# A planner's durations replaced from one point on, and the last attention of a fused fp32 kernel built like its first

## The chip, the cores and the metric

The kernel runs on one core of one Trainium2 chip. The core has a matmul engine (TensorE, PE in the profile, with its weight loads shown apart as PEld), a vector engine (VectorE, DVE), a scalar engine (ScalarE, ACT), GpSimd (POOL) and SyncE (SP), which here issues transfers. Each engine works through its own instructions strictly in order and waits on semaphores for the others. The metric is the device time of one execution in microseconds (us); a lower one is better.

## The reference, cut to what matters

Three layers in fp32, for 2 batches of 448 positions and a model width of 768. The first is causal attention with 12 heads of width 64; the second an MLP with spatial gating; the third, called the last attention here, has 4 experts, each a causal attention head of width 64 of its own, of which each position takes the best two, weighted by a gate.

```python
# first attention, per batch and head
a = exp(scores - max); a = a / (sum(a) + 1e-9); x = a @ v
# gated MLP
h = gelu(x @ w_in); u, v = halves of h;  v_n = layernorm(v) * g_ln
v_s = einsum('ts,bsd->btd', w_sg, v_n) + b_sg
x = x + (u * v_s) @ w_out
# last attention
logits = x @ w_gate;  w = softmax over the 2 largest logits
for e in range(4):
    q, k, v = x @ wq[e], x @ wk[e], x @ wv[e]
    a = causal softmax of q @ k.T / 8
    ye = a @ v @ wo[e]
    out += (w of e, 0 where e isn't among the two) * ye
```

## The kernel before, in words

**Precision.** Big products are made of three: an fp32 number is split into a high half, which the fast fp32r path of the matmul engine takes exactly (xh, gh, wqh), and a low half, the rest (xl, gl, wql); hi x hi + hi x lo + lo x hi are added up in PSUM (`mm3`, L820). `halves` (L613) makes the pair: a copy into hi (L371 on ACT, L373 on DVE or L375 on POOL) and a subtraction into lo (L378, on DVE or POOL). Scores and the first attention's products are plain fp32 matmuls.

**Stages.** The first attention fills the first part of the span. Then come the v chains (x @ w_in for the half that is normalised) and u chains (L859), the spatial product (`spatial`, L1042: 8 tiles of four matmuls at L1053, then on each tile a DVE step with gain and bias at L1056, a multiplication by u at L1059, which DVE or POOL may do, and the halves gh, gl), the product with w_out (`wout_chain`, L1065: 12 tiles of 12 matmuls, then on each a sum with the residual's high half at L1074 on DVE, with its low half at L1077 on DVE or POOL, and the halves of the new x, again xh, xl), and the last attention: `proj_v` (values and gate logits together, 260 columns), `proj_qk`, `scores3` (L1302; two heads side by side, two banks each), the softmax of a bank, the product with v, and `wo_chain` (L1341) with the output transfers.

**The two attentions differ.** `bank_chain` (L417) serves both. Of a bank of scores it takes masked negated scores and their row minimum on DVE (L427), then exp on ACT (L437). In the first attention (`split` false) exp also sums each row; POOL adds 1e-9 (L443), DVE takes the reciprocal (L445), DVE or POOL scales P (L449, L451), the matmul engine transposes the four 128 x 128 blocks (L455), a copy brings them to SBUF (L458), and `pair_chain` (L481) multiplies with v as weight (L497), which gives y already transposed, for two heads in one PSUM tile. In the last attention (`split` true) P is cut into two fp16 halves, `pn` (POOL L471, DVE L473), a DMA transposes both (`dma_start_transpose`, L476) into `pt`, and `out_chain` (L509) multiplies with P as weight and v in fp16 halves with a column of ones for the row sums (L516, L518, L520: 30 matmuls a head). It is normalised and gated in PSUM (L531 to L547), and `y_split` (L551) transposes y back on the matmul engine (L557) and makes its halves. v for it is scaled by its largest element (`v_scales`, L567, with a matmul by a matrix of ones at L576) and split (`v_split`, L593).

**What sets the order.** A planner in Python (`class Order`) builds the instruction streams. A piece of work is a chain of `Step`s; each step has a cost for every engine that may do it (from functions such as `vec(n)`, `pool2(n)` at L61 to L82), marks that it needs and buffers that it takes from rings. `begin` picks for each step the engine on which it would end first by these costs, plus a bias per engine (`BIAS`, and `LATE` after the planned time `TURN`, L221); `run` emits the step that can start first, with the ranks in `R` (L276) deciding between steps within a slack of 60 ns. So costs, biases and ranks decide both which engine does a step and where it stands in that engine's queue.

Of the kernel before, what the change touches and what calls it, by code (L numbers as in the profile page):

```python
# [12 lines left out]
F16 = mybir.dt.float16  # L13
# [5 lines left out]
P = 128  # L19
B, H, S, D = 2, 12, 448, 64  # L20
DM = 768
# [6 lines left out]
PSC = 2.0 ** 14  # L28
MASK = -8.0e9
VW = 132  # L30

SLOTS = ((0, 3, 1, 2), (3, 0, 2, 1))
FLIPS = ((1, 0, 3, 1, 1), (2, 4, 2, 2, 2), (3, 3, 1, 1, 3), (0, 5, 1, 1, 1), (4, 5, 1, 1, 2), (4, 7, 1, 1, 3), (0, 7, 0, 1, 0))
# [4 lines left out]

# [9 lines left out]
TERMS = [  # L50
    (1, 0, 0, 1), (1, 0, 1, 0), (2, 0, 1, 4), (2, 0, 2, 1), (2, 0, 3, 2),
    (0, 1, 0, 0), (3, 1, 0, 4), (3, 1, 1, 1), (3, 1, 2, 2), (3, 1, 3, 3),
]
# [6 lines left out]

def act(n, sb=True, ap=False):  # L61
    return (94 if sb else 51) + 93 * ap + n / 1.2


def mm(n):
    return 2 + n / 2.4


def vec(n):
    return 69 + n / 0.96  # L70


def vec2(n):
    return 69 + n / 1.92


def pool1(n):
    return 56 + n / 0.96


def pool2(n):
    return 150 + 2.1 * n  # L82
# [20 lines left out]
def dma_t(ns, take=(), need=()):  # L103
    return Step({"S": 1244}, take, need, ns, 625)


# [4 lines left out]
class Order:  # L111
# [13 lines left out]
    LATE = dict(T=0, A=300, V=700, G=-300, S=0, Z=0)  # L125
    TURN = 190000
# [68 lines left out]
    def begin(self, ch):  # L195
# [13 lines left out]
        for e, c in st.cost.items():  # L209
# [11 lines left out]
            bias = self.LATE[e] if t > self.TURN else self.BIAS[e] * min(1.0, t / 20000)  # L221
# [55 lines left out]
    PV=(564, 568), PV0=569.5, vp=(569.5, 557.4), gt=(557.3, 543.0), QK=(555.5, 558.9, 570, 579.5),  # L277
    S=(552.4, 561, 560.3, 566.6), WO=(665.7, 669.3), WO0=669, v=(511, 517), v0=509, sp=(526, 538.7),
# [14 lines left out]
def attention_moe_kernel(  # L293
# [21 lines left out]

    uid = [0]
# [19 lines left out]
    ones128 = ct([P, P], F32, "ones128")  # L336
    V.memset(ones128, 1.0)
# [51 lines left out]
    def subs(n):  # L389
        return dict(V=vec(n), G=pool2(n))  # L390


    class Core:


        def __init__(self, stack, side, n, np32, npn, npt):
# [8 lines left out]
            self.split = npn > 0  # L405
            if npn:
                ring("pn" + n, [ct([P, 1024], F16, f"pn{n}{i}", pool) for i in range(npn)])
                ring("pt" + n, [ct([P, 8, P], F16, f"pt{n}{i}", pool) for i in range(npt)])
            else:
                ring("pt" + n, [ct([P, 8, P], F32, f"pt{n}{i}", pool) for i in range(npt)])  # L410
                ring("sm" + n, [ct([P, 4], F32, f"sm{n}{i}", pool) for i in range(4)])
                for _, _, t in o.rings["sm" + n]:
                    G.memset(t, 1.0)
            ring("bias" + n, [ct([P, 4], F32, f"bias{n}{i}", pool) for i in range(6)])
            ring("r" + n, [ct([P, 4, 1], F32, f"r{n}{i}", pool) for i in range(4)])

    def bank_chain(c, key, bank, s, pts, pt_of=None):  # L417
# [7 lines left out]
        _, tm, bias = yield op(V=690, take=("tm" + c.n, "bias" + c.n))  # L425
# [6 lines left out]
        if not c.split:  # L432
            _, p32, sm = yield op(A=1000, take=("p32" + c.n, "sm" + c.n))
        else:
            _, p32 = yield op(A=800, take=("p32" + c.n,))
        for n, (i, rs, cs) in enumerate(parts):
            A.activation(p32[rs, cs], tm[rs, cs], AF.Exp, bias=bias[rs, i : i + 1], scale=-1.0,  # L437
                         **({} if c.split else dict(accum_out=sm[rs, n : n + 1])))
        give("tm" + c.n, tm)
        give("bias" + c.n, bias)  # L440
        if not c.split:
            yield op(G=230)
            G.tensor_scalar(sm[:, 0:2], sm[:, 0:2], 1.0, 1e-9, op0=ALU.mult, op1=ALU.add)  # L443
            yield op(V=160)
            V.reciprocal(sm[:, 0:2], sm[:, 0:2])  # L445
            e, = yield op(kind="pr", G=950, V=500)
            for n, (i, rs, cs) in enumerate(parts):
                if e == "V":
                    V.tensor_scalar(p32[rs, cs], p32[rs, cs], sm[rs, n : n + 1], None, op0=ALU.mult)  # L449
                else:  # L450
                    G.tensor_scalar(p32[rs, cs], p32[rs, cs], sm[rs, n : n + 1], 0.0, op0=ALU.mult, op1=ALU.add)  # L451
            give("sm" + c.n, sm)
            _, t = yield op(T=440, take=(BT,))
            for blk, to in enumerate(SLOTS[bank]):
                T.transpose(t[:, to * P : to * P + P], p32[:, blk * P : blk * P + P], ident)  # L455
            give("p32" + c.n, p32)
            pt = yield from pt_of()
            e, = yield Step(copies_ps(512), kind="pt")  # L458
            copy(e, pt.rearrange("p (a s) q -> p a s q", s=4)[:, :, 2 * bank : 2 * bank + 2, :],
                 t.rearrange("p (a s q) -> p a s q", a=2, s=2))  # L460
            give(BT, t)
            pts["pt"] = pt
            done(("p", key, bank))
            return
        e, pn = yield Step(copies(512), ("pn" + c.n,), kind="hi")
        if e == "A":
            A.mul(pn[:, :512], p32, PSC)
        elif e == "V":
            V.tensor_scalar(pn[:, :512], p32, PSC, None, op0=ALU.mult)
        else:  # L470
            G.tensor_scalar(pn[:, :512], p32, PSC, 0.0, op0=ALU.mult, op1=ALU.add)  # L471
        yield op(V=vec(512))
        V.scalar_tensor_tensor(pn[:, 512:], p32, PSC, pn[:, :512], op0=ALU.mult, op1=ALU.subtract)  # L473
# [3 lines left out]
        give("pn" + c.n, pn)  # L477
        pts[bank] = pt
# [29 lines left out]

    def out_chain(c, key, pts, vv, sv, cv, gate, need, y32_of, after):  # L509
        _, y = yield op(T=970, take=(BY,), need=[("p", key, 0), ("p", key, 1), *need])  # L510
        for n, (i, bk, blk, j) in enumerate(TERMS):
            pt = pts[bk]
            o_ = i * 68
            hi, lo = pt[:, blk, :], pt[:, 4 + blk, :]
            vhi, vlo = vv[:, j, 0:65], vv[:, j, 66:130]
            T.matmul(y[:, o_ : o_ + 65], lhsT=hi, rhs=vhi, start=(n == 0), stop=False,  # L516
                     skip_group_check=True)
            T.matmul(y[:, o_ : o_ + 64], lhsT=hi, rhs=vlo, start=False, stop=False,  # L518
                     skip_group_check=True)
            T.matmul(y[:, o_ : o_ + 65], lhsT=lo, rhs=vhi, start=False,  # L520
                     stop=(n == len(TERMS) - 1), skip_group_check=True)
        for bk in range(2):
            give("pt" + c.n, pts[bk])
        after()
        y4 = y[:, : 4 * 68].rearrange("p (i n) -> p i n", n=68)

# [927 lines left out]
```

## Time and profile before

| | |
|---|---|
| median of 3 runs | 315.57 us (314.58 to 316.84) |
| profiled execution | 315.39 us |
| its span in the trace | 313.3 us |
| PE busy | 295.6 us, 94% |
| POOL busy | 211.9 us, 68% |
| DVE busy | 194.8 us, 62% |
| ACT busy | 169.0 us, 54% |
| mean granted TensorE clock | 0.987 of full speed |

The span is what the trace covers, from the first to the last instruction; 2.09 us of the profiled execution's time lie around it. Busy shares are means over stages with different limits.

### The profile page before, as it was taken

Reading aid. Unit: us, or ns where it says so; the run is one execution under the profiler, and the core shown is the slowest. Engines: PE = TensorE matmul, PEld = TensorE weight load, DVE = VectorE, ACT = ScalarE, POOL = GpSimd, SP = SyncE. Lnnn points to the kernel's source line nnn. Section 1 sums busy time; section 2 is a strip of 40 time slices with the busy share of each in tenths; the row PEclk is TensorE's granted clock in tenths of the full one; section 3 lists DMA queues with packets and bytes.
Section 4 is the critical chain, followed back from the end, with each engine's and each line's share of the span. In section 5 each row is a group of like instructions: output and inputs, shape, how many; then the busy total and the mean of one; then the engine's idle time right before and its main releaser. Section 6 shows DMA issues by size and latency. Waiting matters only on the chain.

```text
span 313.3 us, 6233 instructions
## 1 busy us (share of the span) xinstructions
PE 295.6 (94%) x2076; PEld 232.5 (74%) x2076; DVE 194.8 (62%) x595; ACT 169.0 (54%) x442; POOL 211.9 (68%) x379
## 2 busy tenths in 40 slices
PE   6799999999999999999999999799979999999894
PEld 6467676766666888897886556699958899887793
DVE  3866876999869756334877842156952561858510
ACT  2778989888989753225664310122213363654543
POOL 4679877797868887546669799889995330463510
PEclk9789999999999999999999999999999999999999
DMA  7999556417101034116333000023210640029846
GB/s 212 205 229 223 129 134 180 116 50 212 67 4 58 13 134 119 34 34 179 71 113 93 19 19 0 0 50 69 69 40 27 121 82 18 1 54 132 154 154 201
DMA packets 55184, 29.91 MB, mean 95 GB/s; under 512 B 42800, under 2 KB 52592, under 8 KB 55152
## 3 DMA queue, kind: packets, MB, share of 16 engines
q1 hardware_dynamic: 55152, 29.52, 39.4%
q8 instruction: 16, 0.26, 0.4%
q14 instruction: 16, 0.13, 0.2%
HBM read 22.43 MB, written 2.75 MB: 80 GB/s over the span
## 4 chain that ended last, share of the span: by engine, by line
PE 44%; POOL 26%; DVE 10%; DMA 10%; issue 5%; ACT 3%; SPq 1%; POOLq 0%; ACTq 0%; DVEq 0%
PE bank L820 16%; PE bank L497 5%; PE bank L859 5%; PE bank L775 4%; POOL xl L378 4%; PE bank L455 4%; PE bank L1341 3%; PE bank L1302 3%; DMA raw<-in_moe_w_in_dram 3%; POOL big L1059 3%; POOL big L1077 2%; POOL gl L378 2%; POOL p L451 2%; DVE p L449 2%; DMA qraw<-in_q_dram 2%
## 5 line engine op out<-in xcount | busy, mean ns | idle before, releaser
L437 ACT ACTIVATE p<-tm,bias 128x192 f32<-128x192 f32 (+3 forms) x128 | 61.9, 504 | 9.6 <-DVE bias L427 9.5
L451 POOL TENSOR_SCALAR p<-p,sm 128x192 f32<-128x192 f32 (+1 forms) x88 | 45.6, 531 | 5.7 <-DVE sm L445 4.9
L427 DVE CUSTOM_DVE_ANT_0 tm<-bank,maskw 128x448 f32<-128x448 f32 (+2 forms) x96 | 39.3, 436 | 1.8 <-ACT p L437 1.3
L775 PE MATMUL bank<-kt,qt 64*128 64x128 f32 (+4 forms) x240 | 32.8, 399 | 2.1 <-ACT kt L371 2.1
L455 PE MATMUL bank<-ident,p 128*128 128x128 f32 x192 | 29.6, 285 | 2.1 <-POOL p L451 1.2
L775 PEld LDWEIGHTS bank<-kt,qt 64*128 64x128 f32 (+1 forms) x240 | 16.8, 193 | 15.2 <-issue 10.5
L371 ACT COPY pt<-bank 128x512 f32<-128x512 f32 x41 | 23.3, 587 | 8.3 <-PE bank L455 8.0
L497 PE MATMUL bank<-pt,v_raw 128*64 128x128 f32 (+3 forms) x336 | 27.4, 315 | 0.0
L455 PEld LDWEIGHTS bank<-ident,p 128*128 128x128 f32 x192 | 20.9, 142 | 8.7 <-POOL p L451 4.6
L497 PEld LDWEIGHTS bank<-pt,v_raw 128*64 128x64 f32 x336 | 19.7, 137 | 8.3 <-issue 5.2
L1053 PE MATMUL bank<-wsg,vn 128*128 128x448 f32 x56 | 21.7, 539 | 0.0
L471 POOL TENSOR_SCALAR pn<-p 128x512 f16<-128x512 f32 x15 | 10.4, 698 | 16.2 <-DMA pt<-pn 9.4
L427 DVE CUSTOM_DVE_ANT_0 tm<-bank,mask 128x192 f32<-128x192 f32 x32 | 11.2, 349 | 16.1 <-PE bank L1302 12.0
L833 DVE TENSOR_TENSOR big<-big,bank 128x448 f32<-128x448 f32 (+1 forms) x15 | 9.7, 652 | 17.5 <-POOL big L831 15.9
L649 DVE SCALAR_TENSOR_TENSOR raw<-raw 128x384 int32<-128x384 int32 (+1 forms) x22 | 15.5, 710 | 5.8 <-POOL raw L647 5.6
L820 PE MATMUL bank<-gh,wuh 128*128 128x448 f32 x48 | 18.1, 377 | 1.0 <-ACT gh L371 1.0
L437 ACT ACTIVATION_READ_ACCUMULATOR p<-tm,bias 128x1 f32 x96 | 18.7, 194 | 0.0
L820 PE MATMUL bank<-gl,wuh 128*128 128x448 f32 x48 | 17.9, 372 | 0.7 <-POOL gl L378 0.5
L1053 PEld LDWEIGHTS bank<-wsg,vn 128*128 128x128 f32 x56 | 10.7, 190 | 10.1 <-issue 9.8
L859 PE MATMUL bank<-xh,wuh 128*128 128x448 f32 x48 | 18.0, 375 | 0.0
L859 PE MATMUL bank<-xl,wuh 128*128 128x448 f32 x48 | 17.8, 371 | 0.0
L859 PE MATMUL bank<-xh,wul 128*128 128x448 f32 x48 | 17.6, 371 | 0.0
(208 smaller groups left out, 837.4 us busy)
## 6 DMA issues: line engine op xcount, KB each, us to landing
raw<-in_moe_w_in_dram SPq DMA_DIRECT2D x8, 384.0 KB, 6.2
raw<-in_moe_w_in_dram SPq DMA_DIRECT2D x6, 512.0 KB, 4.1
raw<-in_moe_w_out_dram SPq DMA_DIRECT2D x8, 384.0 KB, 3.1
qraw<-in_q_dram SPq DMA_DIRECT2D x12, 224.0 KB, 4.5
kraw<-in_k_dram SPq DMA_DIRECT2D x12, 224.0 KB, 4.3
v_raw<-in_v_dram SPq DMA_DIRECT2D x18, 128.0 KB, 4.5
out_dram<-v3r SPq DMA_DIRECT2D x3, 384.0 KB, 3.4
raw<-in_moe_w_sg_dram SPq DMA_DIRECT2D x2, 392.0 KB, 4.0
```

Of the source, the lines that this page charges most:

```text
L371: A.copy(dst, src)
L378: (V if e == "V" else G).tensor_sub(dst, a, b_)
L427: V.tensor_tensor_reduce(out=tm[rs, cs], in0=s[rs, cs], in1=masks[i][rs], scale=-0.125, scalar=3.0e38, op0=ALU.add, op1=ALU.min, accum_out ...
L437: A.activation(p32[rs, cs], tm[rs, cs], AF.Exp, bias=bias[rs, i : i + 1], scale=-1.0, **({} if c.split else dict(accum_out=sm[rs, n : n + ...
L451: G.tensor_scalar(p32[rs, cs], p32[rs, cs], sm[rs, n : n + 1], 0.0, op0=ALU.mult, op1=ALU.add)
L455: T.transpose(t[:, to * P : to * P + P], p32[:, blk * P : blk * P + P], ident)
L497: T.matmul(out_, lhsT=x[:, j, :], rhs=rhs, start=(n == 0), stop=(n == len(FLIPS) - 1), skip_group_check=True)
L649: V.scalar_tensor_tensor(low, low, 29, high, op0=ALU.logical_shift_right, op1=ALU.bitwise_or)
L775: T.matmul(s[:m, c0 + c : c0 + c + n], lhsT=qt[rows, QCOL[i] : QCOL[i] + m], rhs=kt[rows, k0 : k0 + n], start=True, stop=True)
L820: T.matmul(o_, lhsT=a, rhs=b_, start=(i == 0), stop=(i == n - 1))
L859: T.matmul(t[:, :S], lhsT=ks[0][a], rhs=ks[1][b_], start=(c == 0 and i == 0), stop=(c == NC - 1 and i == 2))
L1053: T.matmul(t[:, :S], lhsT=vn[b][i][:, fs], rhs=w[:, ts_], start=(j == 0), stop=(j == 3))
```

## The change

It has two parts. **The durations**: from the point at which the first attention's result is complete (`PHASE[0] = 1` in `open_c2`), the planner's cost functions return other, mostly larger numbers, `LATE` holds other biases from there on in place of those behind `TURN`, and the ranks of the last attention's steps are changed. **The last attention** is built as the first: exp sums the rows, P is multiplied by 1/sum and by the gate in one instruction, the matmul engine transposes it in fp32, and `pair_chain` multiplies it with v3r, in fp32, as weight. The fp16 halves, the DMA transposes, the scaling and splitting of v, `out_chain` and `y_split` go.

```diff
+def at(*by_phase):
+    return by_phase[PHASE[0]]
 def act(n, sb=True, ap=False):
-    return (94 if sb else 51) + 93 * ap + n / 1.2
+    return at((94 if sb else 51) + 93 * ap, (193 if sb else 160) + 196 * ap) + n / 1.2
 def mm(n):
-    return 2 + n / 2.4
+    return at(2, 13) + n / 2.4
 def vec(n):
-    return 69 + n / 0.96
+    return at(69, 147) + n / 0.96
 def vec2(n):
-    return 69 + n / 1.92
+    return at(69 + n / 1.92, 130 + n / 1.76)
 def pool1(n):
-    return 56 + n / 0.96
+    return at(56 + n / 0.96, 150 + n / 1.08)
 def pool2(n):
-    return 150 + 2.1 * n
+    return at(150 + 2.1 * n, 200 + 2.12 * n)
...
-    LATE = dict(T=0, A=300, V=700, G=-300, S=0, Z=0)
-    TURN = 190000
+    LATE = dict(T=0, A=100, V=100, G=0, S=0, Z=0)
...
-            bias = self.LATE[e] if t > self.TURN else self.BIAS[e] * min(1.0, t / 20000)
+            bias = self.LATE[e] if PHASE[0] else self.BIAS[e] * min(1.0, t / 20000)
...
-    PV=(564, 568), PV0=569.5, vp=(569.5, 557.4), gt=(557.3, 543.0), QK=(555.5, 558.9, 570, 579.5),
-    S=(552.4, 561, 560.3, 566.6), WO=(665.7, 669.3), WO0=669, v=(511, 517), v0=509, sp=(526, 538.7),
+    PV=(556.5, 563), PV0=556, vp=(569.5, 557.4), gt=(557.3, 543.0), QK=(555.5, 558.9, 562, 564),
+    S=(552.4, 557, 560.3, 563), WO=(665.7, 669.3), WO0=669, v=(511, 517), v0=509, sp=(526, 538.7),
...
     def subs(n):
-        return dict(V=vec(n), G=pool2(n))
+        return dict(V=vec(n) + at(0, 0.3 * n), G=pool2(n))
...
-    def bank_chain(c, key, bank, s, pts, pt_of=None):
+    def bank_chain(c, key, bank, s, pts, pt_of, gate=None, need=()):
...
+        e, = yield op(kind="pr", G=950, V=500, need=need)
+        for n, (i, rs, cs) in enumerate(parts):
+            x, r = p32[rs, cs], sm[rs, n : n + 1]
+            if gate is not None:
+                (V if e == "V" else G).tensor_scalar(x, x, r, gate[rs, i], op0=ALU.mult, op1=ALU.mult)
...
-        _, pt = yield dma_t(896, ("pt" + c.n,))
-        nc.sync.dma_start_transpose(pt, pn)
...
     def open_c2():
         yield wait(*[("x", b, c) for b in range(B) for c in range(NC)])
+        PHASE[0] = 1
...
-        st["core"] = Core(ctx, "left", "3", 3, 3, 6)
+        st["core"] = Core(ctx, "left", "3", 3, 4)
...
+    def pair3(b, pe):
+        yield wait("open")
+        keys = [(b, 2 * pe + i) for i in range(2)]
+        yh, yl = (st["y3" + x][pe][:, b * S : b * S + S] for x in "hl")
+        yield from pair_chain(st["core"], b, keys, [pts3[k] for k in keys], [st["v3r"][b][:, e] for _, e in keys],
+                              [("lg", b, j) for j in range(4)], lambda: yh, lambda: yl, ("y3", b, pe), lambda: None)
```

The scaling step now needs the batch's gates (`need`), which before were first used behind the product with v. The output tiles (`open_ot`) get two tiles of their own where v3r was used again. P goes through a ring of 3 tiles (`p32`) in both kernels.

**Where it moves instructions.** Up to the v chains the matmul engine's order is the same, and from there to the spatial stage it differs by two matmuls that change places. On POOL, between the spatial and the w_out product, before (gh_f and gl_f are the halves of spatial tile f, big the tile that is worked on):

```order
285 L1059 TENSOR_TENSOR big_117<-big_117,u_0_2_114 128x448
286 L375 TENSOR_SCALAR gh_2_1991<-big_117 128x448
287 L378 TENSOR_TENSOR gl_2_1992<-big_117,gh_2_1991 128x448
288 L1059 TENSOR_TENSOR big_118<-big_118,u_0_3_115 128x448
289 L375 TENSOR_SCALAR gh_3_1993<-big_118 128x448
290 L378 TENSOR_TENSOR gl_3_1994<-big_118,gh_3_1993 128x448
```

On DVE at the same place, from the last spatial tile into the w_out tiles, now (L922, L925, L366, L371, L940, L943 are L1056, L1059, L373, L378, L1074, L1077 of before):

```order
433 L922 SCALAR_TENSOR_TENSOR big_117<-bank_97,g_half,b_half 128x448
434 L925 TENSOR_TENSOR big_117<-big_117,u_1_3_1530 128x448
435 L366 CAST gh_3_1994<-big_117 128x448
436 L371 TENSOR_TENSOR gl_3_1995<-big_117,gh_3_1994 128x448
437 L990 MEMSET eidx 128x1 x4
438 L940 TENSOR_TENSOR big_116<-bank_91,xh_73 128x448
439 L943 TENSOR_TENSOR big_116<-big_116,xl_79 128x448
440 L366 CAST xh_73<-big_116 128x448
441 L371 TENSOR_TENSOR xl_79<-big_116,xh_73 128x448
442 L940 TENSOR_TENSOR big_114<-bank_92,xh_73 128x448
443 L366 CAST wkh_2117<-raw_102 128x256
444 L943 TENSOR_TENSOR big_114<-big_114,xl_79 128x448
```

So the gating multiplications and the halves of six of the eight spatial tiles went from POOL to DVE, as did 11 of the 12 sums at L1077, eleven casts and five low halves of x. POOL keeps in the x stage one such sum, seven low halves of x and eight of weights.

On the matmul engine in the last attention, before (S of a pair of heads, the transpose of y of an earlier pair, then the fp16 products, each with its own weight load):

```order
1247 L1302 MATMUL bank_93<-k_2478,q_2476 128x320
1248 L1302 MATMUL bank_94<-k_2478,q_2476 128x320
1249 L557 MATMUL bank_96<-ident,y_2479 128x128 x4
1250 L1302 MATMUL bank_100<-k_2478,q_2476 128x448
1251 L1302 MATMUL bank_98<-k_2478,q_2476 128x448
1252 L1302 MATMUL bank_100<-k_2478,q_2476 64x64
1253 L1302 MATMUL bank_98<-k_2478,q_2476 64x64
1254 L516 LDWEIGHTS pt_2456
1255 L516 MATMUL bank_97<-v3s_1_2143,pt_2456 128x65
```

On the matmul engine now, at the scores of batch 0's second pair (L1158 is L1302 of before, L439 is L455, L465 is L497):

```order
1017 L1158 MATMUL bank_98<-k_2444,q_2442 128x320
1018 L1158 MATMUL bank_95<-k_2444,q_2442 128x320
1019 L439 MATMUL bank_91<-ident,p_2410 128x128 x4
1020 L1158 MATMUL bank_92<-k_2444,q_2442 128x448
1021 L1158 MATMUL bank_94<-k_2444,q_2442 128x448
1022 L1158 MATMUL bank_92<-k_2444,q_2442 64x64
1023 L1158 MATMUL bank_94<-k_2444,q_2442 64x64
1024 L465 MATMUL bank_93<-pt_2416,v3r_2128 64x384
1025 L465 MATMUL bank_93<-pt_2417,v3r_2128 64x384
```

A transpose of P for each of the 16 banks now stands in the matmul engine's queue, between scores, projections and `wo` products, and the product with v takes what these transposes and the copies behind them give.

## Rows read from the trace of the kernel before

**Rows 1.** Window, its length; busy us of PE, PEld, DVE, ACT, POOL; clock, DMA.

```profile
120.00:168.00 48.00, 47.20 (x223) 39.82 (x221) 27.46 (x50) 22.45 (x41) 29.77 (x56) 1.00 0.33 88
...
192.30:224.40 32.10, 30.38 (x145) 26.83 (x144) 17.38 (x27) 7.34 (x17) 29.37 (x44) 1.00 0.18 43
224.40:240.00 15.60, 13.46 (x83) 11.72 (x84) 6.73 (x9) 2.38 (x6) 13.48 (x18) 1.00 0.12 38
240.00:278.00 38.00, 38.00 (x253) 33.46 (x249) 22.87 (x114) 19.29 (x45) 13.68 (x15) 1.00 0.24 46
278.00:309.00 31.00, 28.82 (x366) 25.37 (x365) 13.95 (x46) 16.18 (x41) 9.63 (x14) 1.00 0.70 142
```

**Rows 2.** The chain that ended last: start, us, engine, tile, line.

```profile
198.38 1.10 POOL big L1059
...
233.33 1.17 POOL xl L378
...
282.97 0.59 PE bank L557 x4
...
302.56 6.26 PE bank L1341 x36
```

**Rows 3.** Timeline of PE, w_out product and behind: start, us, [idle before, releaser].

```profile
192.49 0.37 PE L820 MATMUL bank<-gl,wuh 128*128 128x448 f32 x1
...
200.12 0.47 PE L820 MATMUL bank<-gh,wuh 128*128 128x448 f32 x1 [1.01 <-ACT gh L371]
...
201.30 0.37 PE L820 MATMUL bank<-gh,wuh 128*128 128x448 f32 x1
...
224.44 0.28 PE L820 MATMUL bank<-wvh,xh 128*128 128x260 f32 x1
...
228.52 0.36 PE L820 MATMUL bank<-xh,wqh 128*128 128x448 f32 x1
...
234.54 0.47 PE L820 MATMUL bank<-xl,wqh 128*128 128x448 f32 x1 [0.77 <-POOL xl L378]
```

**Rows 4.** Timeline of PE, fp16 products of two heads of the last attention.

```profile
278.00 0.20 PE L516 MATMUL bank<-v3s,pt 128*128 128x65 f16 x1
...
279.84 0.45 PE L820 MATMUL bank<-xl,wkh 128*128 128x448 f32 x1
```

**Rows 5.** Timeline of POOL, a spatial tile and part of the x stage.

```profile
187.67 0.56 POOL L375 TENSOR_SCALAR gh<-big 128x448 fp32r<-128x448 f32 x1
188.31 1.13 POOL L378 TENSOR_TENSOR gl<-big,gh 128x448 fp32r<-128x448 f32 x1
189.40 1.13 POOL L1059 TENSOR_TENSOR big<-big,u 128x448 f32<-128x448 f32 x1
...
213.02 1.16 POOL L378 TENSOR_TENSOR xl<-big,xh 128x448 fp32r<-128x448 f32 x1
```

**Rows 6.** Timeline of DVE: one cast, then part of the x stage.

```profile
127.38 0.30 DVE L373 CAST wvh<-raw 128x260 fp32r<-128x260 f32 x1 [2.66 <-DMA raw<-in_moe_w_gate_dram]
...
210.17 0.62 DVE L1077 TENSOR_TENSOR big<-big,xl 128x448 f32<-128x448 f32 x1
210.71 0.62 DVE L1074 TENSOR_TENSOR big<-bank,xh 128x448 f32<-128x448 f32 x1
212.04 0.42 DVE L378 TENSOR_TENSOR wkl<-raw,wkh 128x256 fp32r<-128x256 f32 x1 [0.71 <-ACT wkh L371]
...
213.03 1.63 DVE L1077 TENSOR_TENSOR big<-big,xl 128x448 f32<-128x448 f32 x1
```

**Rows 7.** DVE's groups by form, 190 to 300: count, busy us, mean ns, idle before.

```profile
L1074 DVE TENSOR_TENSOR big<-bank,xh 128x448 f32<-128x448 f32 x12 | 7.3, 615 | 4.3 <-PE bank L820 4.3
...
L1056 DVE SCALAR_TENSOR_TENSOR big<-bank,g_half,b_half 128x448 f32<-128x448 f32 x2 | 1.4, 684 | 4.6 <-POOL gl L378 2.3 <-PE bank L1053 2.3
```

**Rows 8.** Timeline of PE in the first attention.

```profile
82.02 2.29 PE L497 MATMUL bank<-pt,v_raw 128*64 128x384 f32 x28
84.24 0.66 PE L455 MATMUL bank<-ident,p 128*128 128x128 f32 x4
```

More of the change, by code (lines that the diff above doesn't have):

```diff
@@ L439, in bank_chain @@
         give("tm" + c.n, tm)
         give("bias" + c.n, bias)
[L441 to L464, printed above, removed]
@@ L476, in bank_chain @@
-        nc.sync.dma_start_transpose(pt, pn)
-        give("pn" + c.n, pn)
-        pts[bank] = pt
+        yield op(G=230)
+        G.tensor_scalar(sm[:, 0:2], sm[:, 0:2], 1.0, 1e-9, op0=ALU.mult, op1=ALU.add)
+        yield op(V=160)
+        V.reciprocal(sm[:, 0:2], sm[:, 0:2])
+        e, = yield op(kind="pr", G=950, V=500, need=need)
[3 more added lines that the diff above has]
+                (V if e == "V" else G).tensor_scalar(x, x, r, gate[rs, i], op0=ALU.mult, op1=ALU.mult)
+            elif e == "V":
+                V.tensor_scalar(x, x, r, None, op0=ALU.mult)
+            else:
+                G.tensor_scalar(x, x, r, 0.0, op0=ALU.mult, op1=ALU.add)
@@ new lines, in bank_chain @@
+        give("sm" + c.n, sm)
+        _, t = yield op(T=440, take=(BT,))
+        for blk, to in enumerate(SLOTS[bank]):
+            T.transpose(t[:, to * P : to * P + P], p32[:, blk * P : blk * P + P], ident)
+        give("p32" + c.n, p32)
+        pt = yield from pt_of()
+        e, = yield Step(copies_ps(512), kind="pt")
+        copy(e, pt.rearrange("p (a s) q -> p a s q", s=4)[:, :, 2 * bank : 2 * bank + 2, :],
+             t.rearrange("p (a s q) -> p a s q", a=2, s=2))
+        give(BT, t)
@@ L507, in pair_chain @@
         done(mark)
[L509 to L525, printed above, removed]
-        e, r = yield op(kind="r", V=190, A=250, take=("r" + c.n,))
-        if e == "V":
-            V.tensor_scalar(r, y4[:, :, 64:65], sv, cv, op0=ALU.mult, op1=ALU.add)
-        else:
-            A.activation(r, y4[:, :, 64:65], AF.Identity, bias=cv, scale=sv)
-        yield op(V=94)
-        V.reciprocal(r, r)
-        if gate is not None:
-            yield op(V=73)
-            V.tensor_mul(r, r, gate)
-        y32 = yield from y32_of()
-        e, = yield op(kind="y", V=335, A=264)
-        rb = r.broadcast_to([P, 4, 64])
-        if e == "V":
-            V.tensor_mul(y32, y4[:, :, 0:64], rb)
-        else:
-            A.copy(y32, y4[:, :, 0:64])
-        give(BY, y)
-        if e == "A":
-            yield op(G=pool2(256))
-            G.tensor_mul(y32, y32, rb)
-        give("r" + c.n, r)
-        done(("y", key))
@@ L1206, in gates_chain @@
         done(("gates", b))
-    def v3_prep(b):
-        yield wait(*[("lg", b, j) for j in range(4)])
-        vr, am, sc, cv = (st[n][b] for n in ("v3r", "v3am", "v3sc", "v3cv"))
-        yield from v_scales(E, st["vabs"], vr, am, sc, cv, ("v3sc", b))
-        for pe in range(2):
-            yield from v_split(vr[:, 2 * pe : 2 * pe + 2], sc, st["v3s"][b][pe])
-            done(("v3", b, pe))
     def proj_v(b, j):
```

167 lines of the change are left out of this document (36 added, 131 removed).

## The prediction, made before the changed kernel ran

> **What bounds the kernel now.** I read the busy shares first: PE is at work for 94% of the span, so what counts is PE's instructions and the few places where PE stands. The windows say where these are [rows 1]: 1.7 us without a PE record in the w_out product (32.10 - 30.38), 2.1 us in the stretch behind it, none from 240 to 278, 2.0 us from 278 to PE's end. The granted clock is 1.00 in all of them, the 2.4 GHz level. The chain of waits, read second, names the engine in the first two places: POOL's gating multiplication at 198.38 and POOL's low half of x at 233.33 [rows 2].
>
> Busy records hide part of a loss, because a matmul that follows a wait is longer in the record (0.47 instead of 0.36 us). So I count by starts. In the w_out product 112 matmuls (one has no record) start from 201.30 to 224.44 [rows 3], 0.2066 us apart; the product has 144, the second starts at 192.49, and without a wait the last would end at 192.49 + 143 x 0.2066 = 222.0. It ends at 224.4: **2.4 us lost**, most of it around the wait at 200.12. Behind it PE needs 34 products for v at 0.12 us (224.44 to 228.52), then projections at 0.2008; by that count **2.8 us** are lost up to 234.54, where PE waits for xl, POOL's.
>
> From 222.0 on, PE's work at its dense spacing is 77.2 us: 126 products for v and the gates (15.1), 144 for q and k (28.9), scores 8.8, fp16 products 7.4 (240, 60 of them in 279.84 - 278.00 = 1.84 us [rows 4]), the transposes of y 4 x 0.59 = 2.4 [rows 2], wo 14.6. That is 299.2, and PE ends at 302.56 + 6.26 = 308.82 [rows 2]: 9.6 lost, 2.4 and 2.8 as above and **4.4 in the last attention**, of which 2.0 is open idle time, some 0.4 the two matmuls by the matrix of ones, and the rest the joints between kinds of matmul. Behind PE's end come the last copy and transfer, 4.5 us to the end of the span, and 2.1 around it.
>
> **The change, part by part.** *Stages up to the spatial product*: PE's order is the same but for two matmuls, and from 120 to 168 it has 0.8 us to give back at most [rows 1], so nothing; the spatial product is 8 tiles of 3.0 us by PE and ends at 192.3 in both [rows 3].
>
> *w_out product.* The late wait came from POOL, which takes 0.56 + 1.13 + 1.13 = 2.8 us for a spatial tile [rows 5], and is at that for 29.4 of 32.1 us [rows 1]. On DVE the same tile costs 0.68 for the gain and bias [rows 7], 0.62 for the product (the same form as L1077, 0.62 at 210.17 [rows 6]), about 0.48 for the cast (0.30 for 260 columns [rows 6], scaled by columns) and 0.62 for the low half: 2.4 us, less than PE's 3.0. The last tile's low half is then there at about 194.8. PE first asks for that tile's high half 17 matmuls into the product, at 192.3 + 17 x 0.2066 = 195.8. So the wait goes: **-2.4 us**. What is late next there is the low half by 1.0 us, so this term is safe to about 1 us.
>
> *x stage.* What left POOL must pass DVE: 12 sums at L1074 (0.615 each [rows 7], 7.4), 11 at L1077 (6.8), 11 casts (5.3), 5 low halves (3.1), and of the weights one cast and four subtractions (0.30 and 0.42 [rows 6]: 2.0), together 24.6 us from 194.9 on. POOL has 8 x 1.13 + 8 x 0.75 = 15.0 us there (1.13 as for gl [rows 5], 256 columns in proportion with a fixed part). If they ran freely beside each other, DVE would follow PE's tiles (2.48 us each) and be done about 2.3 us behind the last. They don't: at 213.03 a sum at L1077 that began beside POOL's subtraction of 213.02 took 1.63 instead of 0.62 us [rows 5, 6]. If everything on DVE that reads SBUF alone excludes POOL, the two engines need 24.6 - 7.4 + 15.0 = 32.2 us from 194.9, which ends at 227.1. PE asks for the last halves of x at 222.0 + 28 x 0.12 + 16 x 0.20 = 228.6. That fits, by 1.5 us: **-2.8 us**.
>
> The Trainium skill (SBUF — State Buffer, section Who interferes with whom) says of this that VectorE and GpSimd share one pair of ports under an exclusive lock, and that a VectorE instruction with at most one operand in SBUF is not held up; by it L1074, which has its first operand in PSUM, stays out of the sum, as taken above. The row of 213.03 agrees with the lock; the mean of 615 ns for all 12 sums at L1074 [rows 7], in stretches where POOL was at work for 9 us in 10 [rows 1], agrees with the exception.
>
> *Last attention, PE's work.* Gone: fp16 products 7.4 and transposes of y 2.4. New: 16 transposes of P. One takes 0.66 in the first attention [rows 8], 0.59 to the next start there, and 0.59 for the same shape at 282.97 [rows 2]: 16 x 0.59 = 9.4. And 4 products of a pair with v as weight, 84.24 - 82.02 = 2.22 us each [rows 8]: 8.9. So +18.3 - 9.8 = **+8.5 us**, and PE's work from 222.0 is 85.7. For joints I add 12 at 0.1 (0.47 against 0.36 in the record [rows 3]): **+1.2**, an estimate between 0 (the joint is in the 0.59 already) and 3.
>
> *Last attention, waits.* The 4.4 us go with their causes (the DMA that transposes P, POOL's multiplication of y, the matmuls by ones). In their place PE's queue now holds 16 transposes, each behind exp with row sums, reciprocal, scaling by DVE or POOL and the gates; behind each of them stand projections, scores and wo products that would have been ready. Following the queues with the durations above, the first transpose stands at 250.0 on PE and the gates of its batch are there at about 248.2; for the second batch 283.1 and 281.4; the pairs' products have margins of 0.2 to 2.8 us, one transpose is 0.3 late. I bound the waits by 0 and by the 4.4 of before, and take 1.5, nearest to the 2.0 of open idle time from 278 on. They are not below zero, since dense PE work cannot shrink by them.
>
> **The sum.** 308.82 - 2.4 - 2.8 + 8.5 + 1.2 - 4.4 + 1.5 = 310.4 for PE's end. The output behind the last wo product is the same: + 4.5 + 2.1 = **317.0 us**, +1.6 against the profiled run's 315.39, which is 0.2 below the median of 315.57. A measurement of this kernel tells a change from none at about 1%: 312.4 and 318.7.
>
> **Rivals.** *The lock costs the x stage.* If DVE's sums from PSUM are shut out as well, DVE and POOL in series need 39.6 us from 194.9: 234.5, as late as POOL was before, and 5.9 behind PE's demand. Then 322.9. It decides from 33.7 us of serial work on, that is if only 1.5 us more than I count exclude each other. Against it speaks that sums at L1074 kept 615 ns beside a busy POOL [rows 1, 7]. 10 in 100, slower.
>
> *In-order waits in the last attention.* P's path has three more hops than before ahead of PE, the ring of P has 3 tiles, and a late bank holds up everything on PE. If each of the four pair products or the transposes ahead of it waits 1.3 us, waits are 5.2 and not 1.5: 320.7. From 3.2 us of waits on the time is over 318.7. For it: the margins found are smaller than one POOL instruction (1.13 [rows 5]). Against it: from 240 to 278 PE had no open gap with a longer path [rows 1]. 27 in 100, slower.
>
> *PE's work is smaller than counted.* Four transposes of 128 columns among fp32r products may cost less than 0.59 (0.42 would be 2.7 us less), joints nothing, waits nothing, and the last transfers meet no queue of DMA transposes: 317.0 - 2.7 - 1.2 - 1.5 - 0.6 = 311.0. For it I have no row, only that 0.59 is always seen with a joint. 9 in 100, faster.
>
> *The halves don't come earlier*, because something else of the tile is late: both waits of 5.2 stay in part, 320. 4 in 100.
>
> **How the numbers follow.** My forecast, waits between 0 and 3 and joints between 0 and 2.5, spans 314 to 318.9, with 50 in 100, mostly within 1%, 4 of them slower. Range: down to 313.0, which leaves out the faster rival, and up to 322.0, which takes in the waits and leaves out the full lock. Faster by over 1%: 0.09; within: 0.46; slower: 0.45.
>
> **What would show it.** Right: PE's w_out product dense from 192.3 to 222.0 and no wait at the first projections; DVE busy for nine tenths from 195 to 227; transposes of P 0.59 apart from their next; PE's end at 310. Wrong in the x stage: DVE sums of 1.6 us in a row and PE waiting for DVE's xl. Wrong in the last attention: PE waiting for P (DVE or POOL) ahead of a transpose, or for the copy of P ahead of a product, by more than 3.2 us in all. Wrong in size: starts in the last attention closer than counted.

## The result and the profile after

The changed kernel takes **313.32 us** (median of 17 runs, 311.57 to 314.66), the one before 315.92 (17 runs beside them): ratio 0.9902, 95% interval 0.9876 to 0.9927, 3.1 us less by the ratio. I had forecast 317.0. The time lies at the lower end of the range, on the other side of the kernel before: the sign was wrong. That it is still inside the range is due to the width of the range, not to the sum.

The windows of the changed kernel, columns as in [rows 1]:

```profile
120.00:168.00 48.00, 47.52 (x225) 40.18 (x224) 34.27 (x66) 22.26 (x42) 21.54 (x38) 1.00 0.36 92
...
192.30:224.40 32.10, 32.10 (x165) 29.54 (x164) 30.61 (x51) 4.84 (x12) 18.26 (x20) 1.00 0.23 56
224.40:240.00 15.60, 15.60 (x106) 13.89 (x104) 9.11 (x32) 4.77 (x16) 2.73 (x11) 1.00 0.06 15
240.00:278.00 38.00, 38.00 (x278) 32.50 (x277) 20.74 (x96) 14.83 (x48) 5.17 (x15) 1.00 0.02 4
278.00:309.00 31.00, 30.11 (x215) 26.30 (x213) 13.88 (x51) 14.60 (x40) 4.70 (x11) 1.00 0.22 73
```

From 192.3 on PE is busy in every one of them to its last instruction (the 0.89 us missing in the last lie behind it). DVE and POOL have changed places: 30.6 of 32.1 us on DVE where it was 17.4, POOL 18.3 where it was 29.4. Its timeline on PE, for the points from which the stages are measured (first spatial product, first and last w_out product, first product for v, last wo product; end of the record = start + duration):

```profile
169.05 0.54 PE L919 MATMUL bank<-wsg,vn 128*128 128x448 f32 x1
...
192.75 0.71 PE L685 MATMUL bank<-gh,wuh 128*128 128x448 f32 x1
...
222.08 0.36 PE L685 MATMUL bank<-gh,wul 128*128 128x448 f32 x1
222.28 0.28 PE L685 MATMUL bank<-wvh,xh 128*128 128x260 f32 x1
...
307.77 0.34 PE L1191 MATMUL bank<-woh,y3l 128*128 128x384 f32 x1
```

The points of before that [rows 3] does not show:

```profile
168.23 0.54 PE L1053 MATMUL bank<-wsg,vn 128*128 128x448 f32 x1
...
191.93 0.71 PE L820 MATMUL bank<-gh,wuh 128*128 128x448 f32 x1
...
308.47 0.34 PE L1341 MATMUL bank<-woh,y3l 128*128 128x384 f32 x1
```

The w_out product takes 222.28 - 192.75 = 29.5 us (before 224.44 - 191.93 = 32.5), and from the first product for v to PE's end 308.11 - 222.28 = 85.8 (before 308.82 - 224.44 = 84.4). So 3.0 us were won ahead of the last attention and 1.5 lost in it.

The chain that ended last is now PE's own work from the spatial product on; a few of its rows:

```profile
193.26 41.14 PE bank L685 x217
...
255.57 0.59 PE bank L439 x4
...
257.37 2.22 PE bank L465 x28
...
262.04 0.44 PE bank L439 x4
...
263.09 0.44 PE bank L439 x4
...
298.13 2.22 PE bank L465 x28
300.35 7.78 PE bank L1191 x43
```

41.14 us without a step on another engine, where [rows 2] had two of POOL. A group of four transposes of P (L439) costs 0.59 us only where it stands between score products, 0.44 between other products.

DVE by form, 168 to 235: count, busy us, mean ns.

```profile
L943 DVE TENSOR_TENSOR big<-big,xl 128x448 f32<-128x448 f32 x11 | 9.9, 896 | 0.3
L940 DVE TENSOR_TENSOR big<-bank,xh 128x448 f32<-128x448 f32 x12 | 7.4, 616 | 0.5 <-PE bank L685 0.5
L366 DVE CAST xh<-big 128x448 fp32r<-128x448 f32 x11 | 6.4, 586 | 0.3
...
L366 DVE CAST gh<-big 128x448 fp32r<-128x448 f32 x7 | 2.8, 394 | 1.8 <-POOL big L925 1.6
```

The sum of two SBUF operands (L943) averages 896 ns where it took 0.62 us alone [rows 6], the cast 586 ns where the cast of a spatial tile averages 394, and the sum out of PSUM (L940) is untouched at 616 [rows 7]. The three of these sums with nothing on POOL beside them took 0.61 to 0.63 us, six of the eight others 0.94 to 1.17; the six casts alone 0.38 to 0.39, four of the five others 0.82 to 1.25. Against the times alone the two forms lost 11 x 0.28 + 11 x 0.19 = 5.2 us. DVE still ended the x stage at 226.7, and PE did not wait.

**A measure without the noise of the start.** In all traces, those of the experiments too, the same 1174 records of matmuls stand ahead of the spatial product (some in another order), and PE works without a gap for the last 42.6 us ahead of it. But the point at which it starts moves between 166.5 and 169.2 us from trace to trace. That goes with the granted clock early in the program, where nothing was changed: its mean from 5 to 25 us is 1.00 in the trace that starts at 166.5, 0.91 in the two that start at 166.6 and 166.8, and 0.83 in the others, which start at 167.5 or later (means of the two levels, 2.4 and 1.2 GHz). I therefore compare, beside the medians, **PE's stretch**: from the start of the first spatial product to the end of PE's last. Before: 308.82 - 168.23 = 140.6; after: 308.11 - 169.05 = 139.1.

### The profile page after: what moved, and what is told of

It reads as the page before. It is cut to its first block, busy times and chain, and to the rows that moved or that the text cites. A ratio compares the mean times of both kernels' runs of the same rounds, so it can differ in the third digit from the quotient of the medians.

```text
span 312.4 us, 6008 instructions
## 1 busy us (share of the span) xinstructions
PE 300.1 (96%) x1992; PEld 237.6 (76%) x1992; DVE 221.5 (71%) x656; ACT 162.4 (52%) x450; POOL 161.4 (52%) x319
## 4 chain that ended last, share of the span: by engine, by line
PE 77%; DVE 7%; DMA 6%; POOL 4%; issue 2%; SPq 2%; ACT 1%; POOLq 0%; ACTq 0%; DVEq 0%
PE bank L685 33%; PE bank L465 9%; PE bank L919 8%; PE bank L439 7%; PE bank L640 6%; PE bank L1191 5%; PE bank L724 5%; PE bank L1158 3%; DMA qraw<-in_q_dram 2%; DVE p L433 2%; POOL p L435 2%; PE bank L595 2%; DVE tm L412 1%; DMA raw<-in_moe_w_sg_dram 1%; DMA b_half<-in_moe_b_sg_dram 1%
## 5 line engine op out<-in xcount | busy, mean ns | idle before, releaser
L419 ACT ACTIVATE p<-tm,bias 128x192 f32<-128x192 f32 (+3 forms) x128 | 63.8, 504 | 7.2 <-DVE bias L412 7.1
L435 POOL TENSOR_SCALAR p<-p,sm 128x192 f32<-128x192 f32 (+1 forms) x88 | 46.6, 543 | 6.8 <-DVE sm L426 6.0
L364 ACT COPY pt<-bank 128x512 f32<-128x512 f32 x51 | 29.2, 588 | 23.3 <-PE bank L439 22.9
L439 PE MATMUL bank<-ident,p 128*128 128x128 f32 x256 | 38.7, 283 | 2.3 <-POOL p L435 1.1
L424 POOL TENSOR_SCALAR sm<-sm 128x2 f32<-128x2 f32 x64 | 13.1, 205 | 47.4 <-ACT p L419 43.7
L439 PEld LDWEIGHTS bank<-ident,p 128*128 128x128 f32 x256 | 28.7, 143 | 10.4 <-POOL p L435 4.7
L640 PE MATMUL bank<-kt,qt 64*128 64x128 f32 (+4 forms) x240 | 31.8, 388 | 1.3 <-ACT kt L364 1.3
L465 PE MATMUL bank<-pt,v_raw 128*64 128x128 f32 (+3 forms) x336 | 27.4, 314 | 0.0
L640 PEld LDWEIGHTS bank<-kt,qt 64*128 64x128 f32 (+1 forms) x240 | 16.1, 186 | 14.0 <-issue 10.3
L465 PEld LDWEIGHTS bank<-pt,v_raw 128*64 128x64 f32 x336 | 19.7, 137 | 8.3 <-issue 4.7
L419 ACT ACTIVATION_READ_ACCUMULATOR p<-tm,bias 128x1 f32 (+1 forms) x128 | 24.7, 193 | 0.0
L509 ACT ACTIVATE w<-raw 128x384 f32<-128x384 f32 (+1 forms) x22 | 12.9, 587 | 9.8 <-DMA raw<-in_moe_w_in_dram 5.7
```

The costliest lines, as they stand in the source:

```text
L364: A.copy(dst, src)
L435: G.tensor_scalar(x, x, r, 0.0, op0=ALU.mult, op1=ALU.add)
L465: T.matmul(out_, lhsT=x[:, j, :], rhs=rhs, start=(n == 0), stop=(n == len(FLIPS) - 1), skip_group_check=True)
L640: T.matmul(s[:m, c0 + c : c0 + c + n], lhsT=qt[rows, QCOL[i] : QCOL[i] + m], rhs=kt[rows, k0 : k0 + n], start=True, stop=True)
```

## The experiments

Twelve runs were made: nine other kernels, and three repeats of the two. Three parts of the change can be had apart: D, the durations with the new biases; R, the ranks of the last attention; B, its new build. Each ratio is to the runs of before beside it, which had medians of 315.92, 315.99, 316.56 and 317.30 us.

| run | D | R | B | median us (runs) | ratio to before, 95% | PE's stretch |
|---|---|---|---|---|---|---|
| before | - | - | - | 315.92 (17) | 1 | 140.6, again 143.0 |
| 1 | new | - | - | 313.54 (10) | 0.9926 (0.9891 to 0.9961) | 140.3 |
| 2 | - | new | new | 317.24 (10) | 1.0044 (1.0004 to 1.0084) | 144.7 |
| 5 | new | new | - | 313.15 (5) | 0.9893 (0.9848 to 0.9938) | 139.7 |
| 6 | new | - | new | 314.94 (10) | 0.9945 (0.9912 to 0.9977) | 141.6 |
| 9 | - | new | - | 322.38 (4) | 1.0199 (1.0126 to 1.0272) | 148.4 |
| after | new | new | new | 313.32 (17), again 312.51 (4) | 0.9902, again 0.9874 (0.9807 to 0.9941) | 139.1, 139.0, 139.0 |

The new build alone, with old durations and old ranks, was not run.

**1. Durations only.** The kernel before with the cost functions, `LATE` and `PHASE` of the change.

```diff
+        PHASE[0] = 1
...
-    return 69 + n / 0.96
+    return at(69, 147) + n / 0.96
...
-    LATE = dict(T=0, A=300, V=700, G=-300, S=0, Z=0)
+    LATE = dict(T=0, A=100, V=100, G=0, S=0, Z=0)
```

> The kernel before with the first part of the change alone: the new durations, the new LATE biases and the switch behind the first attention; the last attention and its ranks stay as before (fp16 halves, DMA transposes, P as weight). First theory, from the traces of both kernels: the whole gain of the change is the 2.4 us in the w_out product and the 2.8 us in the x stage, and the new attention costs some 3 us more than the old one; then this kernel beats both, at 315.9 - 5.2 = 310.7 us. Rival: the old attention hangs on its own waits (DMA transposes, v halves), which take back most of what arrives earlier: 313 to 315. Second rival: the durations do nothing by themselves: 315.9.

313.54 us: my first theory fell, the first rival was right. The w_out product takes 29.5 us as in the changed kernel, and most of what is won there is lost again behind it: from the first product for v to PE's end 87.1 us, before 84.4. Who PE waited for, in the whole span from 110 on (total, times, longest):

```profile
PE bank L523 <- DMA pt<-pn: 4.1, 5, 1.6
PE bank L564 <- DVE y L548: 2.4, 2, 1.6
PE bank L1310 <- DVE k L380: 0.8, 1, 0.8
```

Before, the waits of this kind in the last attention were 0.9, 0.4 and 0.6 us. On the chain of waits of this run stand four DMA transposes:

```profile
279.10 3.18 DMA pt<-pn
...
282.64 6.00 DMA pt<-pn x2
...
293.00 4.74 DMA pt<-pn
...
300.50 7.30 PE bank L1349 x42
```

14 of the 21 us ahead of 300.5 are the way of P through the DMA queue: in this trace the end hangs on when the transposes come, not on when x is there. By PE's stretch the gain over before's first trace is only 0.3 us, in the medians it is 2.4. Of the difference 0.8 lies behind PE's end (3.7 us to the end of the span instead of 4.5) and 0.3 around the span (1.8 instead of 2.1); the rest I have not traced.

**2. Attention only.** The changed kernel planned with the old durations and biases (five more lines that go back to before are left out below).

```diff
-    LATE = dict(T=0, A=100, V=100, G=0, S=0, Z=0)
+    LATE = dict(T=0, A=300, V=700, G=-300, S=0, Z=0)
+    TURN = 190000
...
-        PHASE[0] = 1
...
```

> The changed kernel with the old durations, biases and turn: the second part of the change alone. First theory (the attention by itself costs PE some +8.5 - 2.1 + 1.5 us and gives back 4.4 us of old losses and 0.2 behind PE's end, and the two stretches in which PE waited for POOL stay): 315.9 + 3.3 = 319.2 us. Rival, the attention is where the gain is, and the stretches ahead of it do not matter: 313 to 314. Second rival, planned with too small durations the transposes of P stand too early in PE's queue and PE waits there by another 3 us or more: 322 or above.

317.24 us, slower than before by an interval that just leaves out 1; 2 us better than my first theory had it, and neither rival. PE's waits stand at the w_out product (gl 1.4, gh 1.0 us) and at the first projections (xl 0.5); **from the first scores on PE waits for nothing, though it was planned with the small durations.** The w_out product takes 34.3 us: behind the two waits, from 200 to 210, the granted clock is 0.83 (see runs 7 and 8).

**3. Old biases.** The changed kernel with `LATE` of before.

```diff
-    LATE = dict(T=0, A=100, V=100, G=0, S=0, Z=0)
+    LATE = dict(T=0, A=300, V=700, G=-300, S=0, Z=0)
```

> The changed kernel with its new durations, but with the biases that before held late in the program (ACT 300, DVE 700, POOL -300). POOL gets its work back (389 instructions instead of 324). If the shift of work from POOL to DVE is what removes the waits in the w_out product and the x stage, as I hold, both come back: 313.3 + 5 = 318 us, about the time of the kernel with the old durations. If the realistic durations alone do it (the order around the waits), 313 to 314.5.

313.90 us (ratio 0.9936, 0.9900 to 0.9971); I had expected 318. POOL has most of its work back: six of the eight multiplications by u (seven before, two in the changed kernel) and every low half of the spatial tiles and of x. Of the waits of before 0.2 and 0.5 us are left, and the w_out product takes 30.0 us (before 32.5, changed 29.5). In this kernel DVE's first gain and bias, which the first multiplication needs, and POOL's first and last multiplication by u:

```profile
170.37 0.68 DVE L922 SCALAR_TENSOR_TENSOR big<-bank,g_half,b_half 128x448 f32<-128x448 f32 x1
172.04 1.44 POOL L925 TENSOR_TENSOR big<-big,u 128x448 f32<-128x448 f32 x1
...
194.05 1.15 POOL L925 TENSOR_TENSOR big<-big,u 128x448 f32<-128x448 f32 x1
```

Before, the same three:

```profile
176.28 0.65 DVE L1056 SCALAR_TENSOR_TENSOR big<-bank,g_half,b_half 128x448 f32<-128x448 f32 x1
178.99 1.52 POOL L1059 TENSOR_TENSOR big<-big,u 128x448 f32<-128x448 f32 x1
...
198.34 1.13 POOL L1059 TENSOR_TENSOR big<-big,u 128x448 f32<-128x448 f32 x1
```

The spatial product starts at 166.6 here, so POOL is at its first tile 5.4 us into it and through the last multiplication after 28.6. Before, these are 10.8 and 31.2 us behind 168.2. POOL was not too slow for these tiles: once it is at them it takes the same 3.0 us for one in both kernels. It came to them late, and most of that lateness came from DVE, whose first gain and bias starts 8.1 us into the product before and 3.7 here, behind work on weights and on v. Which of the new durations brought it forward was not tried. The shift to DVE is worth some 1 us more (0.6 and 1.4 us by the two medians of the changed kernel, 1.6 by PE's stretch, which is 140.6 here).

**4. Transposes twice.** Each group of four transposes of P in the last attention issued twice.

```diff
-        for blk, to in enumerate(SLOTS[bank]):
-            T.transpose(...)
+        for _ in range(1 if gate is None else 2):
+            for blk, to in enumerate(SLOTS[bank]):
+                T.transpose(...)
```

> The changed kernel with each of the 16 groups of four transposes of P issued twice into the same PSUM tile (same result, planner's costs unchanged). It prices a group by itself. By the prediction's 0.59 us: 313.3 + 9.4 = 322.7 us. By the 0.44 us that the trace of the changed kernel shows between fp32r products: 313.3 + 7.0 = 320.3 us; a group behind its like needs no joint at all, so it may be as low as 0.43. More than 323 would say that the doubled groups also delay what waits for P, and that PE had no cover there.

319.11 us. PE's stretch is 312.81 - 166.84 = 146.0, 6.9 longer than the changed kernel's: 0.43 us a group, whatever stands beside it (the medians differ by 5.8, with the noise of the start in them). Two rows of its chain of waits, a group between score products and one between wo products:

```profile
289.07 1.02 PE bank L440 x8
...
295.49 0.87 PE bank L440 x8
```

A doubled group between score products takes 1.02 instead of 0.59, one between other products 0.87 instead of 0.44: the same 0.43 more. So 0.59 was 0.43 of transposes and 0.16 of joint with the fp32 scores behind it.

**5. Durations and ranks**, the old build.

```diff
-    PV=(564, 568), PV0=569.5, ... QK=(555.5, 558.9, 570, 579.5),
-    S=(552.4, 561, 560.3, 566.6),
+    PV=(556.5, 563), PV0=556, ... QK=(555.5, 558.9, 562, 564),
+    S=(552.4, 557, 560.3, 563),
```

> The kernel before with the new durations and biases (as in the first run) and also with the changed kernel's ranks for the last attention; its build stays the old one. With the durations alone PE waits 7.3 us inside the old attention, the chain of its last 20 us being DMA transposes. If the transposes by DMA are what holds it (16, of 3.2 us each from issue to landing, behind pn and ahead of the product), ranks don't help much: 313 to 314.5. Rival, the old ranks put the last pairs' scores too late and nothing else: the waits go, 310.5 to 311.5, and the new build of the attention is not needed at all.

313.15 us: no measurable difference to the first run, nor to the changed kernel. The waits on DMA transposes fell to 0.4 us, so the ranks did move them, but others came (y from DVE 1.9, the halves of v from POOL 1.4, y from ACT 0.7), and from 280 to 290, behind the wait of 1.9, the granted clock is 0.83. **With the durations and the ranks the old build is as fast as the new one**: it has less work for PE (some 6.4 us, the 8.5 that I forecast less the 2.1 found below) and loses about as much, 5.4 us in open waits and the rest by the clock and in joints.

**6. Old ranks** in the changed kernel: the diff of run 5 turned round.

> The changed kernel with the ranks that the last attention had before. If the ranks are the part of the change that keeps PE free of waits there, these come back, by 2 us or more: 315.5 or above. If the build is (a transpose on PE that comes as soon as P is scaled), the time stays within 0.7 us of the changed kernel: 312.6 to 314.

314.94 us, PE's stretch 2.5 us longer. One open wait of 1.4 us is at a transpose of P, behind the row minimum of its bank; the rest I have not traced to one cause.

**7 and 8. Both kernels again**, for a second trace.

> The kernel before once more, for its trace. From the start of the spatial product to PE's last instruction it took 140.6 us in the trace shown, and that should come back to within 0.3 us; the point at which the spatial product starts (168.2) lay between 166.6 and 169.1 in the six traces so far, and I expect it to move by as much.

> The changed kernel once more, for its trace: 139.1 us from the start of the spatial product to PE's last instruction, within 0.3 us; the start of the spatial product (169.05 in its first trace, the latest of all) between 166.6 and 169.1, more likely near 168.

After: 139.0 us, as expected, with the start at 166.5. Before: 143.0, 2.4 longer than in its first trace, with the same instructions and nearly the same waits. Windows of this second trace of before, columns as in [rows 1], the granted clock last but two:

```profile
195.00:205.00 10.00, 8.05 (x30) 6.24 (x30) 1.91 (x7) 1.18 (x3) 9.02 (x24) 0.88 0.00 0
205.00:215.00 10.00, 10.00 (x49) 9.21 (x49) 5.72 (x9) 2.62 (x6) 8.67 (x10) 0.95 0.17 39
232.00:240.00 8.00, 6.48 (x23) 5.32 (x23) 1.25 (x1) 0.53 (x1) 6.76 (x10) 0.79 0.08 22
```

These are the two places at which PE waited for tiles from POOL. In the first trace the clock stayed at 1.00 there. While it is at the lower level, the w_out matmuls start 0.37 us apart instead of 0.20:

```profile
203.19 0.57 PE L820 MATMUL bank<-gl,wuh 128*128 128x448 f32 x1
203.56 0.57 PE L820 MATMUL bank<-gh,wul 128*128 128x448 f32 x1
```

So these waits can cost twice: once themselves, and once by the clock that falls behind them. Runs 2, 5, 9 and 11 show such falls too, each with a wait of 1.0 us or more just ahead or still under way. In the other traces with waits (the first of before, runs 1, 3, 6 and 10) the clock stayed at 1.00 from the spatial product to PE's end, as it did in the four without any wait (three of the changed kernel, run 4). The times point the same way: of the 55 runs of before beside the experiments that took up to 318.9 us, the twelve over 317.8 us had a mean clock over the whole execution of 0.977 to 0.981; of the 43 shorter ones only four had so little. The 21 timed runs of the changed kernel had 0.982 or more, and none took over 314.66.

**9. Ranks only**, in the kernel before: the diff of run 5 without the durations.

> The kernel before with nothing but the changed ranks of the last attention; old durations, old build. If the ranks act by themselves, as they did with the new durations in the changed build (2.5 us between the traces of the changed kernel and of the one with old ranks), the last attention loses its 4.4 us: 313 to 314. If they only act on a plan whose x stage ends in time, because PE's wait for POOL's halves of x stands ahead of everything they move, 315.5 to 317.

322.38 us, worse than both of my cases. PE's waits, for DMA transposes above all:

```profile
PE bank L516 <- DMA pt<-pn: 5.3, 4, 3.4
PE bank L518 <- POOL v3s L610: 1.9, 1, 1.9
```

The granted clock was 0.83 from 195 to 205 and 0.89 from 278 to 309 there, so a part of the loss is the clock's. Ranks that help one plan by 2.5 us (run 6) cost another 7.8 us of PE's stretch (5.4 against before's second trace, in which the clock fell too).

**10 and 11. Mixed builds.** Durations and ranks new, one batch in the old build, the other in the new. The main lines of run 10 against before; run 11 has `b == 1`.

```diff
-            o.add(rank + i + bank * R['bank3'], bank_chain(st["core"], (b, 2 * pe + i), bank, s, pts3[b, 2 * pe + i]))
+            e = 2 * pe + i
+            more = () if b == 0 else (lambda e=e: pt3_of((b, e)), st["gates"][b][:, :, e : e + 1], [("gates", b)])
+            o.add(rank + i + bank * R['bank3'], bank_chain(st["core"], (b, e), bank, s, pts3[b, e], *more))
```

> A version that the runs point to: new durations, biases and ranks, batch 0 of the last attention in the old build (DMA transposes, fp16), batch 1, which comes last, in the new one. On PE a pair in the old build costs 1.84 + 0.44 to 0.59, in the new one 4 x 0.44 + 2.22, so two pairs save 3.0 us against the changed kernel if nothing waits; the kernel with the old build throughout had 1.8 us of open idle time between 240 and 278, where batch 0 lies. If the waits of the old build come from its place at the end, 310.5 to 312; if they come with it anywhere, 313 or above.

> The mirror of the run before: batch 0 in the new build, batch 1 in the old one, same durations and ranks. The same 3.0 us of PE work less than the changed kernel. If the DMA transposes at the end, beside the output transfers and with little other work for PE left, are what costs the old build its waits, this one keeps them and lands 1 us or more behind its mirror: 312.5 to 314.5. If place doesn't matter, both are equal within 0.5 us.

Batch 0 in the old build: 312.61 us (4 runs, PE's stretch 139.4), between what I expected of either cause; batch 1: 314.76 (10 runs, 141.2). So it matters, by 2 us, which batch keeps the old build; but in neither did the 3.0 us less of PE's work shorten the time. PE's waits with batch 0 in the old build:

```profile
PE bank L527 <- DVE v3s L616: 1.6, 1, 1.6
PE bank L464 <- POOL p L456: 1.1, 2, 0.8
```

With batch 1 in the old build, the longest, on PE's timeline:

```profile
292.93 1.07 PE L566 MATMUL bank<-ident,y 128*128 128x128 f32 x4 [3.11 <-DVE y L550]
```

That the place of the DMA transposes makes the 2 us, as I had expected, these traces don't bear out: PE has no open wait for a DMA transpose in either. With batch 1 it waits 3.1 us for y of the old build's product, from DVE, and the granted clock is 0.83 from 290 to 300, behind that wait; with batch 0 it is 1.00 there.

**12. The changed kernel beside them.**

> The changed kernel once more on the same chip, as the measure for the two mixed builds: 312.5 to 314, and in its trace 139.05 us from the start of the spatial product to PE's last instruction, as in both traces so far.

312.51 us, PE's stretch 139.0. The mixed build is no better; no version here beats the changed kernel by more than the measurement can tell.

## Why the prediction was wrong, point by point

**What bounds it, and the two waits ahead of the last attention: right, with 0.5 us too little for the first.** PE's order up to there, the dense w_out product and no wait for x came as forecast. The product I had ending at 222.0, 30.1 us behind its first matmul's start at 191.93; it took 29.5. The 0.5 us are in the spacing: I had taken 0.2066 us from the matmuls behind the wait at 200.12, but without a wait they start 0.2027 apart, as they do before ahead of its first wait (0.2026 from 192.49 to 197.55). Why that one stretch is wider, no run shows. The reason that I gave for it, that DVE took the tiles over, is not what mattered most: in run 3 the product takes 30.0 us with POOL still at most of them. Less went over, too, than I wrote of the change: of the sums at L1077 six stood on DVE before and 11 now, of the multiplications by u one and six, and of the eleven casts of x POOL had held five and ACT six.

**The lock between DVE and POOL: right in size, and hidden.** I had 32.2 us of work that exclude each other and an end at 227.1; the two forms on DVE lost 5.2 us, and the x stage ended at 226.7, in a trace whose spatial product starts 0.8 us later than before's. The Trainium skill (SBUF — State Buffer, section Who interferes with whom) exempts a VectorE instruction with at most one input in SBUF from the lock, outside the two-port modes, and the 616 ns of the sums out of PSUM agree. The rival in which these sums are shut out as well is false.

**The price of a transpose of P: the first step that failed.** I took 16 x 0.59 = 9.4 us. Both rows that I took it from ([rows 2], [rows 8]) stood ahead of fp32 scores, and 0.16 of each was the joint with them. Run 4 prices a group at 0.43; in the changed kernel 14 groups cost 0.44 and two 0.59, together 7.3. That is 2.1 us too much. I wrote that I had no row for less; the trace of before has some, groups of the same shape ahead of fp16 and of wo products, at 0.47 and 0.41 to the next start:

```profile
291.07 0.63 PE L557 MATMUL bank<-ident,y 128*128 128x128 f32 x4
291.54 0.19 PE L516 MATMUL bank<-v3s,pt 128*128 128x65 f16 x1
...
295.63 0.66 PE L557 MATMUL bank<-ident,y 128*128 128x128 f32 x4 [0.40 <-POOL y L547]
296.04 0.42 PE L1341 MATMUL bank<-woh,y3l 128*128 128x384 f32 x1
```

**The waits in the last attention: the second.** I took 1.5 us, from the 2.0 of open idle time before. There were none, in any of three traces, and none from the scores on in run 2 either, where the planner's durations were wrong. The margins are as thin as I found them by hand (the gates came at 249.5 and the first transposes at 250.6), but a thin margin that holds costs nothing. Of the waits of before, 0.9 us was for a DMA transpose and 0.4 for y on its way back, steps that went with the old build; 0.6 was for k, which the new build has too.

**The joints: mis-sized the other way.** I took 1.2; PE's work by dense spacing is 83.6 us (85.7 less 2.1), and it took 85.8, so 2.2. This is what is left over, not a measurement of joints; some 0.5 of it is that the q and k products start 0.204 us apart on average where I had taken 0.2008.

In all -2.1 - 1.5 + 1.0 in the last attention and -0.5 in the w_out product: -3.1, which takes my +1.6 of PE's end to the -1.5 of PE's stretch. The sign hung on these four. The rival that I gave 9 in 100 had the first two of these steps, and joints of nothing, which the third contradicts.

**The rest of the difference.** PE's stretch gives 1.5 us, the medians 2.6 and their ratio 3.1. I had taken the same 2.1 us around the span for both kernels: it is 2.07 to 2.18 in the runs of before for which the span is on record and 1.73 to 1.92 in the 21 timed runs of the changed kernel, some 0.3 us less; why, no run shows. Behind PE's end it is 4.3, 4.5 and 4.0 us in the three traces of the changed kernel, where I had taken 4.5. And I had no term for the clock that falls behind PE's waits in a part of before's executions. Its price is shown in one trace (2.4 us), and the times fit it; how much of the medians it makes was not measured.

**The parts.** I summed the durations as -5.2 and the attention as +6.8, as if each stood alone. They don't: the durations alone give 2.4 us in the medians, the new build with the new ranks alone costs 1.3, the ranks alone cost 5 or more, and the new build adds nothing measurable to durations and ranks (313.15 and 313.32).

## What to carry to other kernels

Price an operation on a pipelined engine by the start of the next one in a row where its neighbours are those that it will have; a row in which it stands ahead of another kind of product charges the joint to it. Look through the whole trace for such rows before writing that there is none. When an engine that feeds the bound is busy nearly all the time, look at when it comes to the tiles that are waited for, and what it was waiting for itself, before moving work off it. And test the parts of a replanned kernel together as well as apart: ranks that are right for one plan were the worst single change for another.

## What the runs showed of the hardware

- The granted clock can fall behind waits of PE of about 1 us, and need not: means of 0.88 and 0.95 over the windows from 195 to 215, with waits of 0.7 and 1.0 us in the first, and 0.79 from 232 to 240, with two of 0.8 and 0.7, in one of two executions of before with nearly the same waits; its PE stretch was 2.4 us longer. In the other the clock was 1.00 there. At the lower level matmuls of 448 columns on fp32r operands start 0.37 us apart, at the higher 0.20.
- A DVE sum of two SBUF operands took 0.61 to 0.63 us with nothing on POOL beside it and mostly 0.94 to 1.17 with POOL at work, a cast 0.38 to 0.39 and mostly 0.82 to 1.25; a sum with one operand in PSUM 0.61 to 0.63 either way.
- Four fp32 transposes of 128 x 128 cost PE 0.43 us, and 0.59 to the next start when fp32 scores follow.
